# Hedgehog attention and Mish MLP on one core: ScalarE's first copy of the next slot's logits moves between the two halves of the exponentials

## The chip, the cores and the metric
One core of a Trainium2 chip runs the whole program in one launch. The metric is the device time in microseconds (us); the figure for a kernel is the median of its runs.

## The reference
A layer norm of x feeds two branches, and the output is x plus both. Every matrix is bf16; there are 2048 rows of 512.

```python
xn = layernorm(x)                                # 2048 x 512
q, k, v = heads(xn @ wqkv)                       # 32 heads of 16
pq, pk = q @ w_phi[h], k @ w_phi[h]              # logits, 16 per head
phi_q = concat([softmax(pq), softmax(-pq)])      # 32 features per head, phi_k likewise
kv = sum over rows of phi_k^T v                  # 32 x 16 per head
z  = sum over rows of phi_k
o  = (phi_q @ kv) / (phi_q . z + 1e-6)
A  = o @ wo
h  = xn @ w1 + b1                                # 2048 x 1792
B  = (h * tanh(softplus(h))) @ w2                # Mish, then back to 512
out = x + A + B
```

## The kernel before, in words
The 2048 rows are 16 tiles of 128, in four groups of four (`NG = 4`, `TPG = 4`). The weights of the keys and of w_phi are multiplied together beforehand (`fold`), so that one projection of a tile with `wkp` (512 columns) gives its key logits, and one with `wqp` its query logits. `project` (line 156) is four matmuls of 128x512 into one bank of PSUM, and `hidden` (line 178) is four more for one 128-row block of the MLP's first layer, which ScalarE evacuates with the function Mish (line 185).

All these results use the same pool `ps` with five banks, handed out in turn: the sixth request gets the bank of the first, and its first matmul waits until the engine that empties that bank is done. The order of instructions on each engine is the order in which the program is written (`manual_schedule`); nothing is reordered.

The key part runs in slots, the loop over `s` at line 499. Slot `s` finishes the softmax of group `s` and makes the logits of group `s + 1`:

- `exponentials(s, ks)` (lines 227 to 232): ScalarE applies Exp in place to `e`, a 128 x 4096 tile in two halves of 128x2048, one instruction for each half `k`. Half `k` holds the row tiles 2k and 2k + 1 with both signs. Both wait for the last VectorE subtraction of `extremes(s)` (line 220).
- `accumulate(s - 1)` (line 284): 32 small matmuls on TensorE that add the group before into `kv`.
- `value(t, copy)` (line 162): a projection with `wv`, copied to `vext` (line 166). In slots 2 and 3 the first two of a group stand ahead of the logits and are copied by VectorE; the others follow behind and are copied by ScalarE. In slot 1 only the latter two remain, since slot 0 makes the first two in advance.
- `logits(s + 1, i, act)` (lines 192 to 196) for the four tiles `i`: a projection on TensorE, and a ScalarE copy (a CAST in the profile) of its bank into `p_sb`.
- `normalise(s, 0)` and `normalise(s, 1)` (lines 248 to 261): VectorE sums each half of the exponentials, and divides. Group `s + 2` is layer-normed in between.
- In slot 2 `fold` (lines 98 and 108) makes `wqp`.
- `hidden(n)`: 6 + 9, 14, 8 and 10 units in slots 0 to 3; then `extremes(s + 1)` on VectorE.

Slot 0 is written apart: its ScalarE order is Exp of half 0, one copy of logits (line 508), Exp of half 1 (line 509). In slots 1 to 3 both Exps stand together, and the four copies follow behind them. Behind the slots come `second_layer` (line 400), `attend`, `combine` and `project_out` (line 409), which are not touched.

For slot 1 the banks are named here A to E in the order of request: the logits of tiles 4(s + 1) + 0 to 3 are l0 to l3 in A, B, C and D, the two value projections v2 and v3 take E and A again, and the units of `hidden` h1, h2, h3 and so on take B, C, D and on. In slots 2 and 3 two value projections come first, v0 and v1 in A and B: l0, l1 and l2 take C, D and E, l3 takes A, v2 takes B, v3 takes C, and the next request D.

Of the kernel before, what the change touches and what calls it, by code (L numbers as in the profile page):

```python
# [17 lines left out]
def kernel(  # L18
# [16 lines left out]
    TPG = 4  # L35
# [51 lines left out]
    def load_turned(base_col):  # L87

        wT = lnp.tile([P, 4, 512], BF16, name="wT", tag="xn")
        nc.sync.dma_start_transpose(out=wT[:], in_=A_wqkv[:, base_col : base_col + D])  # L90
        return wT

    def fold(wT, dst, dve):

        for kt in range(KT):
            pf = ps.tile([P, 512], FP32, name="pfold", tag="mm")
            for j in range(4):
                nc.tensor.matmul(
                    pf[:, j * P : (j + 1) * P],
                    lhsT=wT[:, j, kt * P : (kt + 1) * P],  # L100
                    rhs=Wbd[:, j, :],
                    start=True,
                    stop=True,
                )
            if kt in dve:
                nc.vector.tensor_copy(dst[:, kt, :], pf[:])
            else:
                nc.scalar.copy(dst[:, kt, :], pf[:])

    def ln_stats(t0, n):  # L110

        stats = lnp.tile([P, TPG, nc.vector.BN_STATS_DIM], FP32, name="stats")
        mv = lnp.tile([P, TPG, nc.vector.BN_AGGR_DIM], FP32, name="mv")
        rstd = lnp.tile([P, TPG], FP32, name="rstd")
        for i in range(n):
            nc.vector.bn_stats(stats[:, i, :], x_sb[:, t0 + i, :])  # L116
        for i in range(n):
            nc.vector.bn_aggr(mv[:, i, :], stats[:, i, :])
        nc.gpsimd.tensor_scalar(
            out=rstd[:, 0:n], in0=mv[:, 0:n, 1], scalar1=1e-5, scalar2=None, op0=ALU.add  # L120
        )
        nc.gpsimd.tensor_tensor(out=rstd[:, 0:n], in0=rstd[:, 0:n], in1=mhalf[:, 0:n], op=ALU.pow)
        return mv, rstd
# [27 lines left out]
    def project(w, t, pp=None):  # L151

        if pp is None:
            pp = ps.tile([P, 512], FP32, name="pproj", tag="mm")[:]
        for kt in range(KT):
            nc.tensor.matmul(  # L156
                pp, lhsT=xnT[:, t, kt, :], rhs=w[:, kt, :],
                start=(kt == 0), stop=(kt == KT - 1),
            )
        return pp  # L160

    def value(t, copy):
        keep(t, project(wv, t), copy)

    def keep(t, pv, copy):
        copy(
            vext[(t // TPG) % 2][:, t % TPG, :, 0:128], pv.rearrange("p (j c) -> p j c", j=4)
        )
# [3 lines left out]
    def hidden(n):  # L172

        for _ in range(n):
            g, f = next(units)
            ph = ps.tile([P, 512], FP32, name="ph", tag="mm")
            for kt in range(KT):
                nc.tensor.matmul(  # L178
                    ph[:],
                    lhsT=w1_sb[:, kt, f * P : (f + 1) * P],  # L180
                    rhs=xnT[:, g * TPG : (g + 1) * TPG, kt, :],
                    start=(kt == 0),
                    stop=(kt == KT - 1),
                )
            nc.scalar.activation(  # L185
                acts[:, f, g * 512 : (g + 1) * 512], ph[:], ACT.Mish, bias=b1f[:, f : f + 1]
            )
# [4 lines left out]
    def logits(s, i, copy):  # L192
        if i == 0:
            p_of[s] = smx.tile([P, TPG, 512], BF16, name="p_sb", bufs=1)
        pp = project(wkp if s < NG else wqp, (s % NG) * TPG + i)
        copy(p_of[s][:, i, :], pp)  # L196
# [30 lines left out]
    def exponentials(s, ks=(0, 1)):  # L227
        for k in ks:
            v = e_of[s][:, 2 * k : 2 * k + 2, :, :]
            nc.scalar.activation(v, v, ACT.Exp)  # L230
            if s >= NG:
                turn(s, k)

    def turn(s, k):

        qT = epool.tile([P, 2, 8, P], BF16, name="qT", bufs=3)
        qT_of[2 * (s - NG) + k] = qT
        for i in range(2):
            nc.sync.dma_start_transpose(
                out=qT[:, i, :, :],  # L240
                in_=e_of[s][:, 2 * k + i, :, :].rearrange("p l c -> p (l c)"),
            )

    def normalise(s, k, between=None):

        v = e_of[s][:, 2 * k : 2 * k + 2, :, :]
        t = smx.tile([P, 128], FP32, name="s")
        nc.vector.reduce_sum(  # L248
            t[:], v.rearrange("p t l (c e) -> p (t l c) e", e=16), axis=AX.X
        )  # L250
        if between is not None:
            between()
        r = smx.tile([P, 128], BF16, name="r")
        r2 = smx.tile([P, 128, 2], BF16, name="r2")
        with nc.allow_low_precision("the softmaxes are bf16"):
            nc.vector.reciprocal(r[:], t[:])  # L256
        nc.vector.tensor_copy(
            r2[:], r[:].rearrange("p (c o) -> p c o", o=1).to_broadcast([P, 128, 2])
        )
        vv = v.rearrange("p t l (c e o) -> p (t l c) e o", e=8, o=2)  # L260
        nc.vector.tensor_tensor(  # L261
            out=vv, in0=vv, in1=r2[:, :, None, :].to_broadcast([P, 128, 8, 2]), op=ALU.mult
        )
# [13 lines left out]
    def accumulate(g):  # L277
        if g == 0:
            kv_of[0] = ps2.tile([P, 3, 512], FP32, name="pkv", tag="kv")
        e = e_of.pop(g)  # L280
        for j in range(4):
            for pl in range(2):
                for i in range(TPG):
                    nc.tensor.matmul(  # L284
                        blocks(kv_of[0], pl, j, 129),
                        lhsT=e[:, i, pl, j * P : (j + 1) * P],
                        rhs=vext[g % 2][:, i, j, 0:129],
                        start=(g == 0 and i == 0 and (j == 0 or (j == 3 and pl == 0))),
                        stop=(g == NG - 1 and i == TPG - 1),
                        skip_group_check=True,  # L290
                    )
# [161 lines left out]
    dve, act = nc.vector.tensor_copy, nc.scalar.copy  # L453
# [31 lines left out]
    def normal(t0, st, xn):  # L485
        ln_apply(t0, TPG, *st, xn, 0)
        for i in (0, 2):
            ln_turn_dma(t0 + i, xn, i)
# [8 lines left out]
    hidden(5)  # L497

    for s in range(NG):
        exponentials(s, (0, 1) if s else (0,))  # L500
        if s > 0:
            accumulate(s - 1)
        if s < NG:
            for i in range(2 if s > 1 else 0):
                value(s * TPG + i, dve)
        if s == 0:
            p_of[1] = smx.tile([P, TPG, 512], BF16, name="p_sb", bufs=1)
            act(p_of[1][:, 0, :], project(wkp, TPG))
            exponentials(0, (1,))
            wide = ps2.tile([P, 3, 512], FP32, name="pwide", tag="kv")  # L510
            for i in range(3):
                project(wkp, TPG + 1 + i, wide[:, i, :])
            ahead = [project(wv, TPG + i) for i in range(2)]
        else:
            for i in range(TPG):
                logits(s + 1, i, act)
        if 0 < s < NG:
            for i in range(2, TPG):
                value(s * TPG + i, act)
        ln = s + 2 < NG  # L520
        if ln:
            t0 = (s + 2) * TPG
            st = ln_stats(t0, TPG)
            xn = lnp.tile([P, TPG, D], BF16, name="xn", tag="xn")
        elif s == 2:
            wT = load_turned(0)

        def amid():
            if s == 0:
                for i in range(2):  # L530
                    keep(TPG + i, ahead[i], dve)
            if ln:
                normal(t0, st, xn)

        normalise(s, 0, amid)
        normalise(s, 1)
        if s == 2:
            fold(wT, wqp, ())
        if s == 0:
            hidden(6)  # L540
            act(p_of[1][:, 1:4, :], wide[:])
        hidden((9, 14, 8, 10)[s])
        extremes(s + 1)
# [78 lines left out]
```

## Time and profile before

| | |
|---|---|
| median of 3 runs | 184.27 us (184.0 to 184.3) |
| the profiled execution's own time | 184.04 us |
| its span | 182.3 us |
| outside the span | 1.74 us |
| busy: TensorE / VectorE / ScalarE / GpSimd | 175.1 / 146.7 / 126.5 / 24.9 us |
| TensorE matmuls | 1039 |
| granted TensorE clock | 1.0 |

In the profile PE is TensorE's matmuls, PEld its weight loads, DVE VectorE, ACT ScalarE, POOL GpSimd and SP the queue that issues most DMAs. Busy shares are averages over the whole span; a bracket at the end of a row of the timeline is the idle time of the engine ahead of that instruction, with the instruction that ended it. All times in the text are from the start of the span.

### The profile page before, as it was taken

To read this page: it belongs to the slowest core of one execution; us is meant where nothing else is said; L and a number is where in the kernel's file an instruction comes from. 1 tells how busy PE (TensorE), PEld (TensorE's weight loads), DVE (VectorE), ACT (ScalarE), POOL (GpSimd) and SP (SyncE) were. 2 spreads that over 40 slices of the span, in tenths; PEclk is the share of its full clock that TensorE was granted. 3 is DMA by queue.
4 is the path that set the end of the run, shared out by engine and by line. 5 is a ranking of instruction groups with operands and counts; after the bars stand their busy time and mean duration, and the time that the engine had idled before them with its cause. 6 is when DMAs were issued, how large, how long until landed. Compare 5 with 4: busy or idle time off the path is not lost.

```text
span 182.3 us, 2759 instructions
## 1 busy us (share of the span) xinstructions
PE 175.1 (96%) x1039; PEld 89.9 (49%) x1039; DVE 146.7 (80%) x255; ACT 126.5 (69%) x194; POOL 24.9 (14%) x30
## 2 busy tenths in 40 slices
PE   6699999999899999999999999999999999999993
PEld 2454344464344645644464555555554545455561
DVE  2989979999999699989999884299926997647963
ACT  2367999987998989979977999273842558235300
POOL 4403079301990000000000000000000000000000
PEclk9999999999999999999999999999999999999999
DMA  6997896300027100000000912943079401990533
GB/s 147 292 407 254 162 347 180 61 4 2 0 58 133 43 0 0 0 0 4 0 0 16 193 26 56 185 104 63 0 165 201 94 6 38 199 194 31 82 94 115
DMA packets 44393, 18.02 MB, mean 99 GB/s; under 512 B 36828, under 2 KB 43868, under 8 KB 44380
## 3 DMA queue, kind: packets, MB, share of 16 engines
q1 hardware_dynamic: 43408, 17.50, 40.3%
q10 hardware_dynamic: 972, 0.35, 0.7%
q8 instruction: 8, 0.13, 0.3%
q14 instruction: 5, 0.04, 0.1%
HBM read 6.84 MB, written 2.10 MB: 49 GB/s over the span
## 4 chain that ended last, share of the span: by engine, by line
PE 73%; DVE 18%; ACT 2%; issue 2%; DMA 2%; DVEq 0%
PE po L400 27%; PE ph L178 17%; PE pproj L156 14%; PE po L409 7%; PE pnd L328 4%; DVE stats L116 4%; PE pkv L284 3%; DVE m L209 3%; DVE s L248 2%; ACT e L230 2%; DVE e L220 2%; DMA x_sb<-in_A_x_dram 2%; DVE e L261 2%; DVE xn L128 1%; DVE r L256 1%
## 5 line engine op out<-in xcount | busy, mean ns | idle before, releaser
L400 PE MATMUL po<-w_sb,acts 128*128 128x512 bf16 (+1 forms) x238 | 50.7, 366 | 0.0
L178 PE MATMUL ph<-xnT,w_sb 128*128 128x512 bf16 x224 | 49.5, 379 | 0.0
L185 ACT ACTIVATE acts<-ph,b1f 128x512 bf16<-128x512 f32 x56 | 35.3, 695 | 2.9 <-PE ph L178 2.7
L178 PEld LDWEIGHTS <-w_sb 128*128 128x128 bf16 x224 | 21.8, 98 | 26.0
L230 ACT ACTIVATE e<-e 128x2048 bf16<-128x2048 bf16 x16 | 29.8, 1903 | 6.7 <-DVE e L220 6.7
L400 PEld LDWEIGHTS <-acts 128*128 128x128 bf16 x238 | 22.8, 98 | 22.2
L156 PEld LDWEIGHTS <-xnT 128*128 128x128 bf16 x192 | 18.3, 98 | 22.7 <-issue 1.3
L417 DVE TENSOR_TENSOR x_sb<-po,x_sb 128x512 bf16<-128x512 f32 (+1 forms) x17 | 10.6, 655 | 12.6 <-PE po L409 12.6
L196 ACT CAST p_sb<-pproj 128x512 bf16<-128x512 f32 x25 | 13.7, 587 | 9.0 <-PE pproj L156 9.0
L248 DVE TENSOR_REDUCE s<-e 128x128 f32<-128x2048 bf16 x8 | 18.2, 2276 | 1.9 <-ACT e L230 1.9
L128 POOL TENSOR_SCALAR xn<-x_sb,mv,rstd 128x512 bf16<-128x512 bf16 x8 | 16.6, 2085 | 0.2
L156 PE MATMUL pproj<-wv,xnT 128*128 128x512 bf16 x64 | 15.1, 379 | 1.1 <-ACT p_sb L196 1.1
L409 PE MATMUL po<-wqk,ob 128*128 128x512 bf16 (+1 forms) x68 | 15.0, 366 | 0.0
L156 PE MATMUL pproj<-wqk,xnT 128*128 128x512 bf16 x64 | 14.5, 379 | 0.0
L337 ACT CAST wkp<-pnd 128x768 bf16<-128x768 f32 x8 | 6.4, 804 | 10.5 <-PE pnd L328 6.5
L209 DVE TENSOR_TENSOR m<-m 128x512 bf16<-128x512 bf16 (+1 forms) x32 | 11.5, 359 | 1.1
L156 PE MATMUL pproj<-wkp,xnT 128*128 128x512 bf16 x52 | 12.1, 379 | 0.0
L209 DVE TENSOR_TENSOR m<-p_sb 128x1024 bf16<-128x1024 bf16 x16 | 11.0, 686 | 1.0 <-ACT p_sb L196 1.0
L337 ACT CAST wv<-pnd 128x768 bf16<-128x768 f32 x8 | 6.4, 794 | 7.3 <-PE pnd L328 5.1
L328 PEld LDWEIGHTS <-qT 128*128 128x128 bf16 x128 | 9.1, 98 | 3.8
L116 DVE BATCH_NORM_STATS2 stats<-x_sb 128x6 f32<-128x512 bf16 x16 | 10.0, 680 | 1.2 <-DMA x_sb<-in_A_x_dram 1.2
L261 DVE TENSOR_TENSOR e<-e,r 128x2048 bf16<-128x2048 bf16 x8 | 10.7, 1337 | 0.3
(67 smaller groups left out, 178.7 us busy)
## 6 DMA issues: line engine op xcount, KB each, us to landing
w_sb<-in_B_w_dram SPq DMA_DIRECT2D x2, 1792.0 KB, 8.8
out_dram<-x_sb SPq DMA_DIRECT2D x15, 128.0 KB, 1.8
x_sb<-in_A_x_dram SPq DMA_DIRECT2D x1, 1024.0 KB, 11.4
x_sb<-in_A_x_dram SPq DMA_DIRECT2D x1, 512.0 KB, 4.2
wv<-in_A_wqkv_dram SPq DMA_DIRECT2D x1, 512.0 KB, 5.1
wqk<-in_A_wo_dram SPq DMA_DIRECT2D x1, 512.0 KB
x_sb<-in_A_x_dram SPq DMA_DIRECT2D x1, 256.0 KB, 3.2
x_sb<-in_A_x_dram ACTq DMA_DIRECT2D x1, 256.0 KB, 3.5
```

Of the source, the lines that this page charges most:

```text
L116: nc.vector.bn_stats(stats[:, i, :], x_sb[:, t0 + i, :])
L128: engine.tensor_scalar(out=xn[:, at + i, :], in0=x_sb[:, t0 + i, :], scalar1=mv[:, i, 0:1], scalar2=rstd[:, i : i + 1], op0=ALU.subtract, ...
L156: nc.tensor.matmul(pp, lhsT=xnT[:, t, kt, :], rhs=w[:, kt, :], start=(kt == 0), stop=(kt == KT - 1),)
L178: nc.tensor.matmul(ph[:], lhsT=w1_sb[:, kt, f * P : (f + 1) * P], rhs=xnT[:, g * TPG : (g + 1) * TPG, kt, :], start=(kt == 0), stop=(kt == ...
L185: nc.scalar.activation(acts[:, f, g * 512 : (g + 1) * 512], ph[:], ACT.Mish, bias=b1f[:, f : f + 1])
L209: nc.vector.tensor_tensor(out=m[:], in0=src[:, :, 0:half], in1=src[:, :, half : 2 * half], op=op)
L230: nc.scalar.activation(v, v, ACT.Exp)
L248: nc.vector.reduce_sum(t[:], v.rearrange("p t l (c e) -> p (t l c) e", e=16), axis=AX.X)
L261: nc.vector.tensor_tensor(out=vv, in0=vv, in1=r2[:, :, None, :].to_broadcast([P, 128, 8, 2]), op=ALU.mult)
L328: nc.tensor.matmul(blocks(pnd, pl, j, 144), lhsT=qT_of[h][:, i, pl * 4 + j, :], rhs=kvm[:, pl, j, :], start=True, stop=True,)
L400: nc.tensor.matmul(po[:, c], lhsT=acts[:, f, t * P : (t + 1) * P], rhs=w2_sb[:, f, c], start=(f == 0), stop=False,)
L409: nc.tensor.matmul(po[:, c], lhsT=oT_of[h][:, t % 2 * 4 + j, :], rhs=wo_sb[:, j, c], start=False, stop=(j == 3),)
```

## The change
In slots 1, 2 and 3 `exponentials(s, (0, 1))` is split: half 0 stays where both were, and half 1 is issued behind the first of the four logits. Only ScalarE's queue is reordered by it: Exp, copy l0, Exp, copies l1 to l3, where it was Exp, Exp, copies l0 to l3. TensorE, VectorE, GpSimd and SP have the same instructions in the same order as before, and the number of ScalarE's instructions and of its table loads stays. What differs for the others is the count of ScalarE instructions that they wait for: the second value projection (v3) now needs the instruction directly behind the first Exp, and VectorE's second sum needs the one behind that copy.

```diff
     for s in range(NG):
-        exponentials(s, (0, 1) if s else (0,))
+        exponentials(s, (0,))
         if s > 0:
             accumulate(s - 1)
         if s < NG:
@@ -512,7 +512,9 @@
                 project(wkp, TPG + 1 + i, wide[:, i, :])
             ahead = [project(wv, TPG + i) for i in range(2)]
         else:
-            for i in range(TPG):
+            logits(s + 1, 0, act)
+            exponentials(s, (1,))
+            for i in range(1, TPG):
                 logits(s + 1, i, act)
```

## The prediction
> **What bounds the kernel now.** The page's busy times come first. TensorE is busy in 96% of the span, so only what takes idle time from TensorE, or adds some, can move the end. The groups by line then say whether TensorE ever waits for the copies that move:
>
> ```profile
> PE 175.1 (96%) x1039; PEld 89.9 (49%) x1039; DVE 146.7 (80%) x255; ACT 126.5 (69%) x194; POOL 24.9 (14%) x30
> ...
> L156 PE MATMUL pproj<-wv,xnT 128*128 128x512 bf16 x64 | 15.1, 379 | 1.1 <-ACT p_sb L196 1.1
> ```
>
> It does, and the list of waits says once, for 1.1 us. The chain that ended last shows the place, and that it is the only hand-over to TensorE after it became the bound:
>
> ```profile
> 43.91 1.89 ACT e L230
> 45.81 0.48 ACT p_sb L196
> 46.29 0.04 issue
> 46.33 1.02 PE pproj L156 x4
> ```
>
> From 46.33 until 178.29 us every piece of this chain is TensorE's. Whatever starts TensorE earlier there reaches the end, unless something else falls due first. Next, the timeline of slot 1, TensorE and then ScalarE (start, length, engine, line, operation):
>
> ```profile
> 40.79 3.62 PE L156 MATMUL pproj<-wkp,xnT 128*128 128x512 bf16 x16
> 44.24 1.03 PE L156 MATMUL pproj<-wv,xnT 128*128 128x512 bf16 x4
> 46.33 1.02 PE L156 MATMUL pproj<-wv,xnT 128*128 128x512 bf16 x4 [1.06 <-ACT p_sb L196]
> 47.19 12.25 PE L178 MATMUL ph<-xnT,w_sb 128*128 128x512 bf16 x56
> ```
>
> ```profile
> 42.10 3.71 ACT L230 ACTIVATE e<-e 128x2048 bf16<-128x2048 bf16 x2 [0.93 <-DVE e L220]
> 45.72 2.03 ACT L196 CAST p_sb<-pproj 128x512 bf16<-128x512 f32 x4
> 47.61 1.11 ACT L166 CAST vext<-pproj 128x512 bf16<-128x512 f32 x2
> 48.74 1.28 ACT L185 ACT_TABLE_LOAD   x1
> 50.03 4.95 ACT L185 ACTIVATE acts<-ph,b1f 128x512 bf16<-128x512 f32 x8
> ```
>
> Sixteen matmuls take 3.45 us (40.79 to 44.24), so four take 0.86. v2 starts at 44.24, and v3 could follow at 45.10. It starts at 46.33, 0.04 after the copy of l0 has emptied bank A (45.72 + 0.57). The lost time, start to start, is 1.23 us; the bracket says 1.06 as it counts from v2's last, pipelined end. Bank A was full from 41.8; ScalarE was in its two Exps.
>
> **What moves.** The price of the new order is read from slot 0, whose ScalarE queue already has it:
>
> ```profile
> 22.94 1.91 ACT L230 ACTIVATE e<-e 128x2048 bf16<-128x2048 bf16 x1
> 24.76 0.57 ACT L508 CAST p_sb<-pproj 128x512 bf16<-128x512 f32 x1
> 25.22 1.91 ACT L230 ACTIVATE e<-e 128x2048 bf16<-128x2048 bf16 x1
> ```
>
> Start to start an Exp takes 1.82 and a copy 0.46, and there is no table load between. In slot 1, Exp to Exp and Exp to copy are 1.81 each (42.10, 43.91, 45.72). So slot 1 becomes, with Exp 0 still at 42.10 (it waits for VectorE's line 220):
>
> - copy of l0 at 43.91, bank A free at 44.48. v3 starts at 45.10 without a wait: 1.23 us gained.
> - Exp 1 at 44.37, copy of l1 at 46.18. That is where l1's copy stands today (45.72 + 0.46), since Exp, copy, Exp add up to the same in either order.
> - h1 needs bank B, which l1's copy empties at 46.18 + 0.57 = 46.75; with the release of 0.04 h1 starts at 46.79. TensorE reaches it at 45.10 + 0.86 = 45.97 and waits 0.82 us: a wait that before was hidden behind v3's.
>
> h1 starts at 46.79, not at 47.19: the gain of slot 1 is **0.40 us**, a third of the wait. Bound from the other side, if l1's copy lasts the 0.59 of the mean row instead, it is 0.38.
>
> The next requests: h2 at 47.65 needs l2's copy (about 47.2), h3 at 48.52 l3's (47.7), h4 and h5 the `vext` copies (48.2, 48.7, against 49.4 and 50.2). h6 at 51.10 needs the first Mish, 50.03 + 0.69 = 50.72, as the table load behind the copies stays at 48.74; Mish repeats every 0.62 us against TensorE's 0.86, so later units are covered too. VectorE's first sum needs Exp 0, unmoved; its second, at 50.13, needs Exp 1, which ends at 46.28 instead of 45.81: 3.8 us spare.
>
> **Slot 2** decides whether the 0.40 is kept, since the copy of l0 can be too early there. TensorE, then ScalarE:
>
> ```profile
> 62.82 3.62 PE L156 MATMUL pproj<-wkp,xnT 128*128 128x512 bf16 x16
> 66.27 1.89 PE L156 MATMUL pproj<-wv,xnT 128*128 128x512 bf16 x8
> ```
>
> ```profile
> 61.48 3.71 ACT L230 ACTIVATE e<-e 128x2048 bf16<-128x2048 bf16 x2
> 65.10 2.03 ACT L196 CAST p_sb<-pproj 128x512 bf16<-128x512 f32 x4
> 67.34 0.59 ACT L166 CAST vext<-pproj 128x512 bf16<-128x512 f32 x1 [0.21 <-PE pproj L156]
> 68.20 0.59 ACT L166 CAST vext<-pproj 128x512 bf16<-128x512 f32 x1 [0.28 <-PE pproj L156]
> ```
>
> Everything 0.40 earlier, Exp 0 starts at 61.08 (VectorE's last subtraction, 59.77 + 1.22, allows 61.02) and ScalarE is ready for l0 at 62.89, but l0 is finished only at 62.42 + 1.03 = 63.45. Here the change **adds a wait** of about 0.6 us on ScalarE. Queued behind it are Exp 1, the copies of l1 to l3, v2 and v3, and `fold`'s four. From l0's end they need 0.03 + 0.46 + 1.81 + 4 x 0.47 = 4.18 until v3's copy could start; v3 itself is finished 5 x 0.86 + 0.03 = 4.35 after l0. So 0.17 us is spare there, and the next reader, h1 (request of the bank that v3's copy empties, at 68.89 today), has some 0.06 more. The idle 0.21 and 0.28 of today cover it: cost **0**, and 0.23 us of cover. VectorE's second sum (68.40) needs Exp 1, which then ends near 65.9.
>
> **Slot 3** has Exp 0 at 79.23 behind VectorE, and l0 ready at 79.34 + 1.03 = 80.37, before the copy's new place at 81.04: no wait. l1's copy stays at 83.31, and h1 there starts at 84.52 with 0.6 us to spare: nothing gained, nothing lost. DMAs are in no queue that moves; the last transposes into `xnT` are issued at 54.6 and land in 3.2 us, well ahead of slot 2. VectorE idles 1.16 us for TensorE at 62.16, so it follows a TensorE that is 0.40 earlier, and with it the rest.
>
> The sum: the wait of 1.23 becomes one of 0.82, by the starts of h1 46.79 - 47.19 = -0.40; slots 2 and 3 add 0. The profiled execution had a span of 182.3 and a time of 184.04 (1.74 around it); it becomes 181.9 and 183.64. It lies 0.23 below the median, so the forecast for the median is 184.27 - 0.40 = **183.87 us**.
>
> **Rivals.** A gain or loss under 0.2% (0.37 us) is about what a measurement of this kernel can't tell from no change, so the forecast lies just beyond that line.
>
> *Slower: switching between Exp and copy costs ScalarE time.* If the two more switches of a slot cost q us together, slot 1 gains 0.40 - q, slot 2 loses q - 0.23 once its cover is gone, and slot 3 loses only beyond 0.6. The change turns to a loss from q = 0.32; at q = 0.5 it is -0.40 + 0.50 + 0.27 = +0.37, 184.64 us. For it: only one place in the trace has this order. Against: that place gives q of 0.01 (1.82 against 1.81). 9 in 100.
>
> *Slower, far: the copy drops the Exp table.* A table load lasts 1.283 us in this trace (twelve times in lines 185 and 230). Two more per slot are 2.57: 2.17 lost in slot 1, 2.34 in slot 2, about 2.0 in slot 3, together 6.5, 190.8 us. Against: no load stands around line 508, nor between Exp and the copies of slots 1 to 3, and the changed program has as many table loads as before. 1 in 100.
> The Trainium skill, "ScalarE: Activation LUTs", section "Table sets: the hidden batching unit", tells authors to batch calls by set, which speaks against an operation between two Exps; it also says that copy is in every set. By the page's 2.66 us for a switch to a different set, six would be 16 us; by the rows above, none occurs.
>
> *No change that can be told:* the 0.82 left at h1 grows to eat the gain (q between 0.1 and 0.4), or VectorE, whose slot 1 does not move, sets slot 2 after all. Against: VectorE's 1.16 idle. 184.27 us, 12 in 100.
>
> *The whole wait goes:* if h1 did not have to wait for l1's copy, 1.23 us would be gained, 183.04. Against: the order of the five banks. 3 in 100.
>
> **The numbers.** The forecast's own case has 75 in 100. Within it the size is known to some 0.1 us, and runs of before differ by 0.3; as 0.40 is little more than 0.37, I put about 0.53 of all chances beyond the line from this case, with the 0.03 of the whole wait 0.56; 0.10 for slower by both mechanisms; 0.34 within. The range takes in the forecast's case with the runs' spread, the unchanged case, and most of the slower one: 183.4 to 184.6.
>
> **What would show it.** In the profile after: v3 straight behind v2, no bracket; a new bracket of about 0.65 to 0.8 us at the first `ph` matmul of slot 1, released by p_sb line 196; h1 at 46.8; in slot 2 a ScalarE wait of about 0.6 ahead of l0's copy, released by TensorE, with no idle TensorE behind it; every later piece 0.40 earlier; twelve table loads. Wrong if h1 starts at 47.2 or later, if TensorE waits in slot 2, or if Exp and copy take longer than 1.82 and 0.46.

## The result, and the profile after

| | before | after |
|---|---|---|
| median (9 runs each) | 184.18 us (183.95 to 184.41) | 183.68 us (183.54 to 183.79) |
| profiled execution: time, span | 184.04, 182.3 us | 183.56, 181.8 us |
| ratio of after to before | | 0.9973, 95% interval 0.9963 to 0.9983 |

The change makes the kernel faster by 0.50 us (0.31 to 0.68 by the interval); 0.40 was forecast. The list of waits of the kernel after (engine, line, waited for; us, times, longest) shows the exchange. The wait of `pproj` for `p_sb` is gone, and one of `ph` for `p_sb` has come; ScalarE's own waits for `pproj` grew from 9.0 to 9.6, one more than before:

```profile
ACT p_sb L196 <- PE pproj L156: 9.6, 13, 4.4
PE ph L178 <- ACT p_sb L196: 0.6, 1, 0.6
```

The timeline of slot 1 after, TensorE and then ScalarE:

```profile
44.17 1.89 PE L156 MATMUL pproj<-wv,xnT 128*128 128x512 bf16 x8
46.70 12.25 PE L178 MATMUL ph<-xnT,w_sb 128*128 128x512 bf16 x56 [0.65 <-ACT p_sb L196]
```

```profile
41.98 1.91 ACT L230 ACTIVATE e<-e 128x2048 bf16<-128x2048 bf16 x1 [0.89 <-DVE e L220]
43.80 0.57 ACT L196 CAST p_sb<-pproj 128x512 bf16<-128x512 f32 x1
44.26 1.91 ACT L230 ACTIVATE e<-e 128x2048 bf16<-128x2048 bf16 x1
46.08 1.55 ACT L196 CAST p_sb<-pproj 128x512 bf16<-128x512 f32 x3
```

v2 and v3 are now one row of eight matmuls without a gap. h1 waits for the copy of l1, which stands at 46.08 and is done at 46.66, and starts 0.04 later. Exp to copy is 1.82 and copy to Exp 0.46, as in slot 0, and the table loads are the same twelve.

The clean measure is from the start of Exp 0 to h1: 47.19 - 42.10 = 5.09 before, 46.70 - 41.98 = **4.72 after**, so 0.37 is the change's own. The other 0.12 of the 0.49 between the two traces lies ahead of slot 1, in Exp 0 itself, where nothing was changed.

In slot 2, ScalarE waits for l0 as foreseen, and VectorE's wait for TensorE shrinks from 1.16 to 0.78. First ScalarE after, then VectorE before and after:

```profile
60.99 1.91 ACT L230 ACTIVATE e<-e 128x2048 bf16<-128x2048 bf16 x1
63.44 0.59 ACT L196 CAST p_sb<-pproj 128x512 bf16<-128x512 f32 x1 [0.55 <-PE pproj L156]
63.93 1.91 ACT L230 ACTIVATE e<-e 128x2048 bf16<-128x2048 bf16 x1
65.74 1.55 ACT L196 CAST p_sb<-pproj 128x512 bf16<-128x512 f32 x3
67.16 1.13 ACT L166 CAST vext<-pproj 128x512 bf16<-128x512 f32 x2
```

```profile
62.16 0.69 DVE L166 CAST vext<-pproj 128x512 bf16<-128x512 f32 x1 [1.16 <-PE pproj L156]
```

```profile
61.66 0.69 DVE L166 CAST vext<-pproj 128x512 bf16<-128x512 f32 x1 [0.78 <-PE pproj L156]
```

ScalarE has caught up at the two `vext` copies: the idle time of 0.21 and 0.28 that stood ahead of them is used up. And TensorE's first `ph` unit of slot 2 is at 68.40 (68.89 before: 0.49 earlier, no wait behind l0). In slot 3 it is at 84.03 against 84.52, 0.49 again.

### The profile page after: what moved, and what is told of

It is laid out like the page before. It is cut to its first block, busy times and chain, and to the rows that moved or that the text cites. A ratio compares the mean times of both kernels' runs of the same rounds, so it can differ in the third digit from the quotient of the medians.

```text
span 181.8 us, 2744 instructions
## 1 busy us (share of the span) xinstructions
PE 175.2 (96%) x1024; PEld 90.1 (50%) x1039; DVE 146.6 (81%) x255; ACT 126.3 (69%) x194; POOL 24.9 (14%) x30
## 4 chain that ended last, share of the span: by engine, by line
PE 73%; DVE 18%; ACT 3%; issue 2%; DMA 2%; DVEq 0%
PE po L400 26%; PE ph L178 17%; PE pproj L156 14%; PE po L409 7%; PE pnd L328 4%; DVE stats L116 4%; PE pkv L284 3%; DVE m L209 3%; DVE s L248 2%; ACT e L230 2%; DVE e L220 2%; DMA x_sb<-in_A_x_dram 2%; DVE e L261 2%; DVE xn L128 1%; DVE r L256 1%
## 5 line engine op out<-in xcount | busy, mean ns | idle before, releaser
L400 PE MATMUL po<-w_sb,acts 128*128 128x512 bf16 (+1 forms) x232 | 50.0, 366 | 0.3
L409 PE MATMUL po<-wqk,ob 128*128 128x512 bf16 (+1 forms) x65 | 14.3, 366 | 0.1
```

What stands on the lines that cost most here:

```text
L400: nc.tensor.matmul(po[:, c], lhsT=acts[:, f, t * P : (t + 1) * P], rhs=w2_sb[:, f, c], start=(f == 0), stop=False,)
L409: nc.tensor.matmul(po[:, c], lhsT=oT_of[h][:, t % 2 * 4 + j, :], rhs=wo_sb[:, j, c], start=False, stop=(j == 3),)
```

## The experiments

All are written on the kernel before, with a choice of how many copies stand between the two Exps in each slot. The times of the first four were compared with 23 runs of before (median 184.01 us), those of the last four with 20 (184.05).

```diff
+        between = (0, a, b, c)[s]
-        exponentials(s, (0, 1) if s else (0,))
+        exponentials(s, (0, 1) if s and not between else (0,))
...
             for i in range(TPG):
+                if between and i == between:
+                    exponentials(s, (1,))
                 logits(s + 1, i, act)
+            if between == TPG:
+                exponentials(s, (1,))
```

**Slot 1 alone** (`a, b, c = 1, 0, 0`).

> Only slot 1 has the new order; slots 2 and 3 are as before. Theory (the gain is slot 1's alone, a TensorE wait of 1.23 us start to start exchanged for one of about 0.82): as much as the whole change, -0.4 us against before, and a TensorE wait of about 0.65 in the profile at the first ph matmul, released by line 196. Rival (slots 2 and 3 give some of it): clearly less than the whole change, about -0.2. Rival (an Exp and a copy in turn cost ScalarE time): from Exp 0 to the copy of l1 more than 4.1 us.

Measured: 183.62 us, ratio 0.9977 (0.9968 to 0.9986): 0.42 faster, as much as the whole change within the intervals. From Exp 0 (42.02) to the copy of l1 (46.12) it is 4.10, no more than was worked out, and from Exp 0 to h1 4.72 again. The bracket is smaller than foreseen because TensorE came later:

```profile
44.52 1.89 PE L156 MATMUL pproj<-wv,xnT 128*128 128x512 bf16 x8
46.74 12.25 PE L178 MATMUL ph<-xnT,w_sb 128*128 128x512 bf16 x56 [0.34 <-ACT p_sb L196]
```

**Slots 2 and 3 alone** (`0, 1, 1`).

> Only slots 2 and 3 have the new order; slot 1 is as before. Theory: 0.0 us against before, the 1.06 us bracket of slot 1 unchanged, a ScalarE wait of about 0.55 ahead of the copy of l0 in slot 2 and no TensorE wait behind it. Rival (slots 2 and 3 give some of the gain): -0.2. Rival (the new ScalarE wait in slot 2 costs time): +0.1 to +0.4 with a TensorE wait in slot 2.

Measured: 183.96 us, ratio 0.9997 (0.9988 to 1.0006): no change that can be told. ScalarE's wait in slot 2 is there, and TensorE shows no wait behind it. In slot 1 h1 stands 46.95 - 41.86 = 5.09 after Exp 0, as in the kernel before. The bracket there was expected at 1.06 and came as 0.63, again because v2 started later:

```profile
44.43 1.03 PE L156 MATMUL pproj<-wv,xnT 128*128 128x512 bf16 x4
46.09 1.02 PE L156 MATMUL pproj<-wv,xnT 128*128 128x512 bf16 x4 [0.63 <-ACT p_sb L196]
46.95 12.25 PE L178 MATMUL ph<-xnT,w_sb 128*128 128x512 bf16 x56
```

**Two copies between, slot 1 alone** (`2, 0, 0`).

> Slot 1 alone, but the copies of l0 and l1 both stand between the two Exps. Theory (what is left at h1 is the wait for l1's copy behind Exp 1): h1 has no wait, l2's copy empties its bank at 47.2 and h2 waits about 0.4 us, h2 starts 0.8 earlier than before; the sixth ph unit then meets the first Mish with next to no margin, so -0.75 to -0.8 us against before. Rival (VectorE sets slot 2 after all): no better than -0.4, as Exp 0 of slot 2 can't start before 61.0.

Measured: 183.54 us, ratio 0.9971 (0.9960 to 0.9981), 0.53 faster. The trace does what was expected: h1 waits for nothing, h2 for l2's copy, 47.20 - 41.99 = 5.21 after Exp 0 against 5.95 before (h1's 5.09 and 0.86):

```profile
44.27 1.89 PE L156 MATMUL pproj<-wv,xnT 128*128 128x512 bf16 x8
45.99 1.03 PE L178 MATMUL ph<-xnT,w_sb 128*128 128x512 bf16 x4
47.20 11.39 PE L178 MATMUL ph<-xnT,w_sb 128*128 128x512 bf16 x52 [0.18 <-ACT p_sb L196]
```

That is 0.74 in the trace; the times give 0.35 to 0.74. This profiled execution took 183.20, the shortest of its seven. The second run of this kernel, below, asks why the others are longer. The rival's condition came true and cost nothing: VectorE lets Exp 0 of slot 2 start only at 60.92, with 0.30 us of ScalarE idle ahead of it, but TensorE's first `ph` unit of slot 2 stands at 68.04, still 0.74 earlier than before when counted from Exp 0 of slot 1.

**The second Exp behind all four copies in slots 2 and 3** (`1, 4, 4`).

> Slot 1 as in the change, and in slots 2 and 3 the second Exp stands behind all four copies. Theory (in slot 2 ScalarE has only 0.23 us of cover after l0 is finished): v3's copy could start 5.36 us after l0's end and not 4.35, TensorE waits about 0.7 in fold and 0.25 at the first ph unit of slot 2, 0.97 together; slot 3 costs nothing, as Exp 0 there waits for VectorE and l0 is ready before it. Together -0.40 + 0.97 = +0.57 us against before. Rival (TensorE's timing in slot 2 does not hang on ScalarE): -0.4, like the change. Rival (slot 3 is as sensitive): above +1.2.

Measured: 184.94 us, ratio 1.0052 (1.0039 to 1.0064): 0.96 slower, more than the 0.57 expected. Slot 2 lost what was worked out. `fold`'s last four matmuls wait for v2's copy, and the first `ph` unit for v3's:

```profile
67.97 0.83 PE L98 MATMUL pfold<-Wbd,wT 128*128 128x128 bf16 x12
69.37 0.38 PE L98 MATMUL pfold<-Wbd,wT 128*128 128x128 bf16 x4 [0.56 <-ACT vext L166]
69.86 7.07 PE L178 MATMUL ph<-xnT,w_sb 128*128 128x512 bf16 x32
```

From Exp 0 of slot 1 (42.45) that unit stands at 27.41; in the kernel after at 26.42. So the loss is 0.99, against 0.97. Slot 3's own units add nothing (43.03 against 42.05, still 0.98). What the expectation missed lies behind that. VectorE's second sum of slot 2 now waits for Exp 1:

```profile
68.88 2.29 DVE L248 TENSOR_REDUCE s<-e 128x128 f32<-128x2048 bf16 x1 [0.42 <-ACT e L230]
```

Counted from Exp 0 of slot 1, VectorE runs 0.51 later from there on than in the kernel after (this row at 26.43 against 25.92), and slot 3 adds nothing to that. Behind the slots ScalarE loses more. The table load ahead of the next Exps waits in this trace until VectorE's last subtraction is done; in the kernel after, it runs while ScalarE would wait for VectorE in any case. This run, then the kernel after:

```profile
97.33 1.28 ACT L230 ACT_TABLE_LOAD   x1 [2.32 <-DVE e L220]
98.62 3.71 ACT L230 ACTIVATE e<-e 128x2048 bf16<-128x2048 bf16 x2
```

```profile
93.56 1.28 ACT L230 ACT_TABLE_LOAD   x1
96.29 3.71 ACT L230 ACTIVATE e<-e 128x2048 bf16<-128x2048 bf16 x2 [1.45 <-DVE e L220]
```

From Exp 0 of slot 1 these Exps stand at 56.17 instead of 54.31, 1.86 later: some 0.5 is VectorE's delay, and most of the rest is the load of 1.28. Why the load waits here isn't shown. ScalarE then runs late through the next Mish units and the copies of `attend`, and TensorE pays 0.26 for it: eight matmuls from 104.63 would end their turn at 106.36, and line 328 starts at 106.62. 0.99 + 0.26 - 0.37 = 0.88 of the 0.96.

**Three copies between, slot 1 alone** (`3, 0, 0`).

> Slot 1 alone, with the copies of l0, l1 and l2 between the two Exps. Counted from the start of Exp 0: l3's copy empties bank D at about 5.65, so h3 has next to no wait; but the table load and the first Mish behind all copies stay where they are, 8.66 counted so, and the sixth unit h6 needs that Mish. Theory (ScalarE's unchanged work between Exp 0 and the first Mish is the floor): -0.75 us, no better than two copies, with the TensorE wait now released by line 185. Rival (only the logits' copies matter): the whole 1.23 us, and no wait by line 185.

Measured: 183.50 us, ratio 0.9966 (0.9953 to 0.9978), 0.63 faster, like two copies. No TensorE wait is left in slot 1: v2 starts at 44.93, 2.65 after Exp 0 (42.28), and h1 directly behind v3 at 46.66. With so late a TensorE, h6 comes at 4.38 + 5 x 0.86 = 8.70, just behind the floor of 8.66. So the run does not tell whether the first Mish or TensorE's own arrival sets the limit, and this stays open.

**Two copies between in all slots** (`2, 2, 2`).

> Two copies between the Exps in all three slots. Theory (in slot 2 the copy of l1 can only start once l1 is finished, 0.86 us after l0, so Exp 1 starts 1.35 us after l0's end and v3's copy 4.57 after it instead of 4.35, with 0.06 of cover left): a TensorE wait of 0.13 to 0.2 us at the first ph unit of slot 2, so 0.13 to 0.2 slower than two copies in slot 1 alone. Rival (slot 2 does not care): the same as two copies in slot 1 alone, and no TensorE wait in slot 2.

Measured: 183.71 us, ratio 0.9980 (0.9970 to 0.9990), between the two runs with two copies in slot 1 alone (0.9971, 0.9964) and before: 0.17 to 0.29 us less gain, which the intervals alone do not separate. The trace shows a loss in slot 2, where l1 isn't ready behind l0, and where h1 then waits for v3's copy (67.67 + 0.62, and 0.04) instead of starting at 67.21 + 0.89 = 68.10:

```profile
63.15 0.59 ACT L196 CAST p_sb<-pproj 128x512 bf16<-128x512 f32 x1 [0.26 <-PE pproj L156]
63.95 0.59 ACT L196 CAST p_sb<-pproj 128x512 bf16<-128x512 f32 x1 [0.22 <-PE pproj L156]
```

```profile
67.21 1.06 PE L98 MATMUL pfold<-Wbd,wT 128*128 128x128 bf16 x16
68.34 3.83 PE L178 MATMUL ph<-xnT,w_sb 128*128 128x512 bf16 x17
```

The difference is 0.24, a little above the 0.13 to 0.2 that were worked out. There is no bracket, as the row of `fold`'s short matmuls is shown up to 68.27; the starts show it.

**Two copies, slot 1 alone, once more** (`2, 0, 0`), and **the changed kernel itself** beside it.

> Two copies in slot 1 alone, once more, for a second trace: the first gave 0.74 us from Exp 0 to h2 in its trace, but 0.53 in the comparison of times. Theory A (TensorE reaches v2 at a time that differs between executions, 2.14 to 2.57 us after Exp 0 in the traces so far, and from 2.62 on its own arrival sets h2): a time about 0.5 below before, and a trace with h2 at the later of 5.21 and v2 + 2.59, counted from Exp 0. Theory B (spread of the comparison): -0.7.

> The changed kernel itself, beside the versions with two and three copies on one chip. Theory: h1 4.72 us after Exp 0 again (5.09 before), -0.4 us against before, and slower by 0.1 to 0.35 than two copies in slot 1 alone. Rival (what two copies gain more is lost elsewhere): the same time as these.

Measured: two copies 183.52 us, ratio 0.9964 (0.9952 to 0.9975), 0.66 faster, which as a time does not decide between the two theories. The trace does: v2 starts at 45.16, 2.94 after Exp 0 (42.22), h1 has no wait, and h2 follows it at 47.75, which is 5.53 after Exp 0 and is v2 + 2.59. So TensorE's own arrival set h2 here, and the gain in this execution is 5.95 - 5.53 = 0.42, not 0.74: theory A.

```profile
45.16 1.89 PE L156 MATMUL pproj<-wv,xnT 128*128 128x512 bf16 x8
46.89 12.25 PE L178 MATMUL ph<-xnT,w_sb 128*128 128x512 bf16 x56
```

The changed kernel: 183.52 us, ratio 0.9975 (0.9965 to 0.9985), 0.46 faster. Its h1 is once more 46.70 - 41.98 = 4.72 after Exp 0, though v2 came 2.99 after it and no wait was left to see:

```profile
44.97 1.89 PE L156 MATMUL pproj<-wv,xnT 128*128 128x512 bf16 x8
46.70 12.25 PE L178 MATMUL ph<-xnT,w_sb 128*128 128x512 bf16 x56
```

The intervals of two copies, three copies and the change overlap and two of the medians are equal. That the change is slower than two copies by 0.1 to 0.35, as was expected, is not shown, nor is any version that beats it, although its traces gain 0.42 to 0.74 where the change's gain 0.37.

Where TensorE's delay comes from can be read in the list of waits of these two runs, first the changed kernel's, then that of two copies. In slot 0, TensorE waits for a DMA transpose into `xnT`:

```profile
PE pwide L156 <- DMA xnT<-xn: 0.8, 1, 0.8
```

```profile
PE pwide L156 <- DMA xnT<-xn: 0.7, 1, 0.7
```

The wait was absent in the trace of before, and in those of after, of the first run with two copies and of the run with all four (v2 at 2.14 to 2.28 after Exp 0); it was 0.3 us in four others (2.50 to 2.65), and 0.7 and 0.8 in these two (2.94, 2.99). The longer of the two `xnT` transposes issued shortly before slot 0 takes 3.7 to 3.8 us from issue to landing in the four traces without the wait, 3.8 to 4.1 in the four with 0.3, and 4.1 and 4.2 in these two.

VectorE, which sets Exp 0, does not share the delay. ScalarE does: its Mish units of slot 0 come later with TensorE, but the idle time ahead of Exp 0 takes that up. It was 0.89 in the first trace of the changed kernel (its bracket stands above); in the second the load ends at 41.89, 0.09 ahead of an Exp 0 that is in the same place:

```profile
40.61 1.28 ACT L230 ACT_TABLE_LOAD   x1
41.98 1.91 ACT L230 ACTIVATE e<-e 128x2048 bf16<-128x2048 bf16 x1
```

## Why the prediction was right

- **The place and the mechanism.** One hand-over, l0's copy to v3's bank in slot 1, was to be moved, with a smaller wait left at h1 by the order of the banks. The profile after has exactly this, and slot 1 alone gives 0.42 against the change's 0.46 and 0.50, slots 2 and 3 alone nothing that can be told.
- **The size.** 0.40 was worked out; from Exp 0 it is 5.09 - 4.72 = 0.37 in every trace of this order in slot 1. The term that was off is the copy of l1 with its Exp: 1.82 + 0.46 + 1.82 + 0.58 + 0.04 = 4.72, where the prediction had 1.81, 0.46, 1.81, 0.57 and 0.04, 4.69. Three comparisons of times (0.50, 0.42, 0.46) lie 0.05 to 0.13 above 0.37, and every interval holds 0.37. From h1 to the end of the span it is 135.1 to 135.2 us before, after, in the second trace of the change and in both runs with only some of the slots, so nothing behind slot 1 adds to the gain; where the rest sits, if it is more than spread, no trace here shows. The median came to 183.68 where 183.87 was forecast: 0.10 of that is the larger gain, and 0.09 that before's own median is 184.18 here and not 184.27.
- **The cover in slot 2.** ScalarE's new wait was put at 0.6 and is 0.55, and the spare 0.23 us behind it held, with little left of it. The run with two copies everywhere went past it and lost 0.24 in slot 2, the one with four lost 0.99.
- **The rivals.** Switching between Exp and copy costs next to nothing: 1.82 and 0.46, as in slot 0, against 1.81 between Exps. No table load was added. The Trainium skill, "ScalarE: Activation LUTs", section "What ACT_TABLE_LOAD costs", has back-to-back ACTIVATEs overlap by about 93 ns; the trace agrees, with an Exp of 1.91 us and the next instruction, copy or Exp, 1.82 after it.
- **What hid the remainder.** The prediction took TensorE's arrival in slot 1 from one trace, as a fixed 2.14 after Exp 0, and so called the wait left at h1 0.82. It is 0.0 to 0.8, as the arrival is 2.14 to 2.99. The gain stood nevertheless, since h1 at 4.72 is set by ScalarE up to an arrival of 4.72 - 1.73 = 2.99, and the old order's 5.09 up to 3.37. That the latest arrival seen is just this limit was luck. It could not have come much later, though: in that trace the table load ends only 0.09 ahead of Exp 0, so a still later TensorE would take Exp 0 with it. By an estimate from these rows v2 comes at most some 3.06 after Exp 0, which would leave a gain of about 0.3.

## What to carry to other kernels

When results share a few banks in turn, look for who empties the next bank as well: putting one evacuation ahead of a long instruction only hands the wait to the second one. The gain is then not the whole bracket but the time that the waiting engine needs for one result less the time of one more copy: here a projection of 0.86 on TensorE less a copy of 0.46 on ScalarE, 0.40, of which 0.37 was measured. Two copies ahead gave twice that, 0.74, where TensorE arrived in time. Measure a gain of this size from the event that sets the chain (here the Exp that waits for VectorE), not from the span's start and not by a bracket's length; and before moving more work ahead, ask whether its input is ready, since a queue that waits for the input of an early copy delays all that stands behind it.

## What had not been expected

TensorE's phase against VectorE and ScalarE at the start of slot 1 varies by 0.85 us between executions with the same instructions on TensorE. It goes with how long TensorE waits in slot 0 for a DMA transpose to land (0 to 0.8 us). The time before hides this, because TensorE waits there for ScalarE in any case; the more copies are moved ahead, the more the gain hangs on it (0.42 to 0.74 us for two copies).
